# The up-projection of the first batch's second half, made as products of quarters

## The chip, the cores and the metric

The kernel runs on one core of one Trainium2 chip. The metric is the device time of one execution in microseconds (us); the time before is 982.87 us, the median of four runs (981.88 to 982.91).

## The reference

Two blocks follow each other. The first is attention with routing: batch 4, 8 heads, 768 positions, head size 64, 16 clusters. Each query and key goes to its nearest centroid, and a query sees only keys of its own cluster. The second takes the result, transposed to 3072 rows of 512, through two weight matrices.

```python
q_assign = np.argmax(np.einsum('bhsd,hcd->bhsc', q_n, c_n), axis=-1)
k_assign = np.argmax(np.einsum('bhsd,hcd->bhsc', k_n, c_n), axis=-1)
mask = q_assign[:, :, :, None] == k_assign[:, :, None, :]
scores = np.where(mask, scale * np.matmul(q, k.transpose(0, 1, 3, 2)), -1e9)
attn = softmax(scores)                  # rows add up to 1
x = np.matmul(attn, v)                  # -> (3072, 512)
h = x @ w_in                            # w_in 512 x 2048
g = h - np.tanh(h)
return g @ w_out                        # w_out 2048 x 512
```

## The kernel before

**Attention.** Heads are worked in pairs: 4 pairs in each of 4 batches, 16 pairs `n`. A pair is done in two halves of 384 queries (`TB`), and a half in three steps of two key blocks. So there are 96 steps. Steps 0 to 11 are the first halves of the first batch's pairs, 12 to 23 their second halves, 24 to 47 the second batch, 48 to 71 the third, 72 to 95 the fourth. The loop over steps writes all engines' instructions in a hand-made order; nothing is moved afterwards. Each engine takes its instructions strictly in that order.

In every step, `begin` issues 8 score matmul instructions for the following step (`sc`, L451) into two PSUM tiles (pool `ps_s`, two buffers) and two `Exp` on ACT, in place. `value` issues 8 matmul instructions of this step's weights with the values (`av`, L505). `select` (L483) makes the weights of the following step on DVE: it multiplies the exponentials, read from PSUM, by the mask "same code"; it is called twice per step with two instructions each. POOL adds the weights up (`sum`, L492 and L496). In one step of six, a new pair is turned (`pt`, L332), compared with the centroids (`sim`, L351) and routed one step later: `route` transposes (`pr`, L364) and makes codes in four DVE instructions, the last two of which need no PSUM. `publish` (L396, L400) writes the codes to DRAM, from where `spread` fetches them as a row. `total_both` (L566) takes the POOL sums of both halves of a pair through PE.

**The feed-forward block as a filler.** Between these, every step takes some items from a list. The list of the batch before is spread over the steps by weights written by hand (2.6 for an `up`, 3.4 for a `project`). After its matmuls, each item calls `between()`, which emits the next part of the step's `todo` list (the two `select`, then routing, publishing, scaling and so on, split evenly over the items).

- First batch (`plain_items`): 16 `up` items for each half, each 8 matmuls (16 instructions in the profile) of 384 columns (L676), a tanh on ACT (L681) and a subtraction on DVE (L683); then 12 `project` items (L692). First half in steps 12 to 23, second half in steps 24 to 47.
- Later batches (`strassen_items`): the weights and the activations are cut into quarters, and seven products of quarters take the place of eight. `up_product` (L871) makes one product of 4 matmuls (8 instructions) of 384 columns. For each of 8 rows `i` of quarters, the products come in the order 1, 2, 6, 7, 4, 5, 3. Product 1 is copied out of PSUM by ACT (L876); the others are added up by DVE (L859), product 5 in two additions. When two results are ready, `shrink` runs tanh on ACT (L864) and a subtraction on POOL (L866).

All filler matmuls, `sim`, `pr`, `pq` and `den` take turns in the same PSUM pool `ps_f` of three buffers. So a product can begin only when the result three places before it was read.

The sums of weight quarters ("factors") are made by DVE (L773: 8 instructions for the up weights, 8 for the down weights) and kept in DRAM by the SP queue (L737, L756); `light` names the steps for that. `open_stream` (step 39) gives the space of `w_in` to three `stream` buffers, and `fetch_factors` (L795, SP) brings back 896 KB for each row `i`. `right_factors` (L832) makes the differences of activation quarters on DVE.

Of the kernel before, what the change touches and what calls it, by code (L numbers as in the profile page):

```python
# [39 lines left out]
P = 128  # L40
# [18 lines left out]
def kernel(  # L59
# [119 lines left out]
    def fast():  # L179
# [178 lines left out]
        def route(n: int):  # L358

            t = sims.pop(n)  # L360
            ps = ps_f.tile([P, TB], F32, name="pr", tag="f")
            for j in range(HCH):
                c = slice(j * P, (j + 1) * P)
                nc.tensor.transpose(out=ps[:, c], in_=t[:, c], identity=ident)  # L364
            G = HCH * 8
            pr = ps.rearrange("p (g c) -> p g c", c=C)
            shape = [P, G, C]
            places = down.unsqueeze(1).to_broadcast(shape)
            mx = rtp.tile([P, G], F32, name="mx")
            nc.vector.reduce_max(out=mx, in_=pr, axis=AX.X)  # L370
            top = rtp.tile(shape, F32, name="top")
            nc.vector.tensor_tensor(  # L372
                out=top, in0=pr, in1=mx.unsqueeze(2).to_broadcast(shape), op=ALU.is_ge
            )
            nc.vector.tensor_tensor(out=top, in0=top, in1=places, op=ALU.mult)
            code = codes[n] = codep.tile([P, 2, 2, 2, HCH], F32, name="code")
            nc.vector.reduce_max(
                out=code.rearrange("p i a h j -> p j (i a h)"),
                in_=top.rearrange("p (j g) c -> p j g c", j=HCH), axis=AX.X,
            )  # L380
# [238 lines left out]
        def spread_out(n: int, half: int):  # L619
            back = lists.pop((n, half))  # L620
            if joined(n):
                pool = late_pools.get("den", sump)
                dens[n, 1] = pool.tile([P, TB], F32, name="den")
                for i in range(2):
                    for h in range(2):
                        nc.sync.dma_start(
                            dens[n, i][h * D : h * D + D], back[i, h : h + 1].to_broadcast([D, TB])
                        )
                return
            for h in range(2):  # L630
                nc.sync.dma_start(
                    dens[n, half][h * D : h * D + D], back[h : h + 1].to_broadcast([D, TB])
                )
# [31 lines left out]
        def plain_items(half: int):  # L665
# [39 lines left out]
            if half == 0:  # L705

                order = [(s, i) for i in range(NQ4) for s in range(2)] + order[2 * NQ4 :]
            return [(2.6, 1, lambda between, f=f: up(f, between)) for f in sequence] + [
                (3.4, 1, lambda between, s=s, i=i: project(s, i, between)) for s, i in order
# [76 lines left out]
        def fetch_factors(n: int):  # L786

            if n < (B - 1) * PER:
                i = n % PER
                t = streams[n] = late_pools["stream"].tile([P, HF, HM], F32, name="stream")  # L790
                if i < HF:
                    t = streams[n] = t.rearrange("p a b -> p (a b)")[:, 0 : 7 * CH * P].rearrange(
                        "p (c k f) -> p c k f", k=7, c=CH
                    )
                nc.sync.dma_start(t, up_factors[i] if i < HF else down_factors[i - HF])  # L795

        late_pools, diffs = {}, {}

        def open_stream():
            first_in.close()  # L800
            late_pools["stream"] = cx.enter_context(
                tc.tile_pool(name="stream_late", bufs=3, side="right", reuse_waits="tile")
            )
            late_pools["den"] = cx.enter_context(
                tc.tile_pool(name="den_late", bufs=1, side="right", reuse_waits="tile")
            )
            for n in range(2):
                fetch_factors(n)

        def open_late():  # L810
            first.close()
            for name, bufs in (
                ("diff", 1), ("u", 2), ("s", 2), ("th", 2), ("g", 1), ("left", 1), ("du", 1),
                ("c", 4), ("raw", 2),
            ):
                late_pools[name] = cx.enter_context(
                    tc.tile_pool(name=name + "_late", bufs=bufs, reuse_waits="tile")
                )
            late_pools["G"] = late_pools["g"].tile([P, HF, 2, 2, TB], F32, name="G")
            late_pools["S1"] = late_pools["left"].tile([P, HF, TB], F32, name="S1")  # L820

        def right_factors(b: int, c: int):

            if c == 0:
                diffs[b] = late_pools["diff"].tile([P, 3, CH, TB], F32, name="diff")
            d = diffs[b]
            x, y = xT[b * HP + c], xT[b * HP + CH + c]
            for out, u, w in (
                (d[:, 0, c], x[:, 1], x[:, 0]), (d[:, 1, c], y[:, 1], d[:, 0, c]),
                (x[:, 1], y[:, 1], x[:, 1]), (d[:, 2, c], y[:, 0], d[:, 1, c]),  # L830
            ):
                nc.vector.tensor_tensor(out=out, in0=u, in1=w, op=ALU.subtract)  # L832

        def strassen_items(b: int):
            base = (b - 1) * PER

            held = {}
            G, left1 = late_pools["G"], late_pools["S1"]

            def up_product(i: int, k_: int, between):  # L840
                which = PRODUCTS[k_]
                x = [xT[b * HP + c] for c in range(CD)]
                d = diffs[b]
                right = {
                    1: [x[c][:, 0] for c in range(CH)], 2: [x[CH + c][:, 0] for c in range(CH)],
                    3: [x[CH + c][:, 1] for c in range(CH)], 4: [d[:, 2, c] for c in range(CH)],
                    5: [d[:, 0, c] for c in range(CH)], 6: [d[:, 1, c] for c in range(CH)],
                    7: [x[c][:, 1] for c in range(CH)],
                }[which]
                if k_ == 0:  # L850
                    held[i] = (
                        late_pools["s"].tile([P, TB], F32, name="s"),
                        late_pools["u"].tile([P, 2, TB], F32, name="u"),
                    )
                s, u = held[i]
                g = G[:, i]
# [4 lines left out]
                def shrink(f: int, halves_=slice(0, 2)):  # L861
                    t = g[:, f, halves_]
                    th = late_pools["th"].tile([P, 2, TB], F32, name="th")[:, halves_]
                    nc.scalar.activation(out=th, in_=t, func=ACT.Tanh)  # L864
                    t, th = (x.rearrange("p a n -> p (a n)") for x in (t, th))
                    nc.gpsimd.tensor_tensor(out=t, in0=t, in1=th, op=ALU.subtract)  # L866

                ps = ps_f.tile([P, TB], F32, name="pu", tag="f")
# [8 lines left out]
                elif which == 2:  # L877
                    add(g[:, 0, 0], ps, s)
                    if i == HF - 1:
                        shrink(0, slice(0, 1))  # L880
# [5 lines left out]
                elif which == 4:  # L886
                    add(g[:, 1, 0], ps, u[:, 1])
                elif which == 5:
                    add(u[:, 0], ps, u[:, 0])
                    add(g[:, 1, 1], ps, u[:, 1])  # L890
                    shrink(1)
                else:
                    add(g[:, 0, 1], ps, u[:, 0])

                    shrink(0, slice(1 if i == HF - 1 else 0, 2))
                between()
                if k_ == len(PRODUCTS) - 1:

                    nc.gpsimd.tensor_tensor(out=left1[:, i], in0=g[:, 0, 1], in1=g[:, 1, 1], op=ALU.add)
                    nc.gpsimd.tensor_tensor(  # L900
                        out=g[:, 0, 1], in0=g[:, 0, 0], in1=g[:, 0, 1], op=ALU.subtract
                    )
                    streams.pop(base + i)
# [3 lines left out]
            def down_product(k_: int, j: int, between):  # L907
# [51 lines left out]

            return [  # L960
                (1.3, 1, lambda between, i=i, k_=k_: up_product(i, k_, between))
                for i in range(HF) for k_ in range(len(PRODUCTS))
            ] + [
# [11 lines left out]
        def before(n: int):  # L975
# [10 lines left out]
            yield lambda: route(n)  # L986
# [7 lines left out]
        ready = {}  # L994
# [68 lines left out]
        route(0)  # L1063
        turn(1, 0, nc.scalar)
# [13 lines left out]
        route(1)  # L1078
        begin(steps[0])
# [23 lines left out]
        for at, (n, half, s) in enumerate(steps):  # L1103
# [4 lines left out]
            if at == 4 * HALF - 9:  # L1108
                open_stream()
            if at in fills:  # L1110
                fill, over = fills[at][0](), fills[at][1]
                whole, spent, since = sum(it[0] for it in fill), 0.0, at
            if at == 2 * HALF:
                makers = [it for i in range(2) for it in up_maker(i)]
                makers += [it for i in range(2) for it in down_maker(i)]
# [71 lines left out]
            todo += [stages[i] for i in (5, 3, 4, 2) if i in stages]  # L1187
            todo += late
# [18 lines left out]
            light = [i for i in range(at, 4 * HALF - 2) if i % 3 and i % 6 != 1]  # L1207
# [8 lines left out]
            slots = max(sum(it[1] for it in now), 1)  # L1216
            place = iter(range(slots))
# [10 lines left out]
            if at in fills and "raw" in late_pools:  # L1228
# [10 lines left out]

        PRS = len(PRODUCTS)  # L1240
        tail = tail[:2] + tail[PRS : PRS + 2] + tail[2:PRS] + tail[PRS + 2 :]
# [218 lines left out]
```

## Time and profile before

| | us |
|---|---|
| median of four runs | 982.87 |
| the profiled execution, whole | 983.38 |
| its span | 981.6 |
| PE busy in the span | 971.7 |
| DVE, POOL, ACT busy | 535.6, 497.2, 316.6 |
| in the chain: first `h` of step 24, first `o` of step 36 | 206.11, 290.29 |

The page gives busy time per engine, and the costliest groups as "busy, mean ns of one". The view of the chain goes back from the last instruction and says in each stretch what work the end waited for. In the timeline, a bracket holds the idle time before an instruction and what ended it. The granted clock of PE is 0.998 over the span.

### The profile page before, as it was taken

The page shows a single profiled execution, that of the slowest core. Times are in us where ns is not written, and L with a number is a line of the kernel's source. Part 1 is how long each engine was busy: PE and PEld are TensorE (multiplying, and loading weights), DVE is VectorE, ACT ScalarE, POOL GpSimd, SP SyncE. Part 2 cuts the span into 40 slices and gives each one's busy share as a digit, 9 for nine tenths or more (in the row PEclk, how much of TensorE's full clock was granted, in tenths as well). Part 3 has the DMA queues.
Part 4 walks back from the last instruction along what each step waited for, and adds up shares of the span by engine and source line. Part 5 has one row for each costly group of instructions (what it writes and reads, how often), then busy time and mean ns, then how long its engine had stood idle before and what let it go on. Part 6 is the DMA issues. An engine that isn't in the chain of part 4 may idle for free.

```text
span 981.6 us, 16550 instructions
## 1 busy us (share of the span) xinstructions
PE 971.7 (99%) x6456; PEld 460.5 (47%) x6456; DVE 535.6 (55%) x1010; ACT 316.6 (32%) x484; POOL 497.2 (51%) x347
## 2 busy tenths in 40 slices
PE   8999999999999999999999999999999999999997
PEld 5433443344443334444455555444455555444664
DVE  6458656447566577647655457655754436543011
ACT  5576554233332333243422222333242121222000
POOL 1026334444445454677686345666688445466600
PEclk9999999999999999999999999999999999999999
DMA  7664452124565633463544646344344132233221
GB/s 204 183 186 144 151 143 94 30 73 132 155 203 167 173 116 110 148 195 99 180 159 157 188 136 201 110 151 149 123 159 135 62 118 95 83 113 129 104 103 35
DMA packets 113385, 132.47 MB, mean 135 GB/s; under 512 B 60388, under 2 KB 93076, under 8 KB 110612
## 3 DMA queue, kind: packets, MB, share of 16 engines
q1 hardware_dynamic: 106916, 109.81, 36.6%
q0 software_dynamic: 6240, 21.50, 6.3%
q8 instruction: 53, 0.87, 0.4%
q14 instruction: 32, 0.26, 0.1%
q10 hardware_dynamic: 144, 0.03, 0.0%
HBM read 110.14 MB, written 21.17 MB: 134 GB/s over the span
## 4 chain that ended last, share of the span: by engine, by line
PE 95%; DMA 2%; DVE 1%; ACT 1%; SPq 0%; issue 0%; POOL 0%; ACTq 0%; DVEq 0%
PE pd L922 22%; PE pu L871 22%; PE sc L451 14%; PE av L505 13%; PE o L692 8%; PE h L676 8%; PE pt L332 2%; PE sim L351 1%; PE den L566 1%; DMA den<-back 1%; PE den L539 1%; PE den L520 1%; PE pr L364 1%; DVE e L483 1%; DMA row<-q_codes 0%
## 5 line engine op out<-in xcount | busy, mean ns | idle before, releaser
L496 POOL TENSOR_TENSOR sum<-sum,e 128x768 f32<-128x768 f32 x112 | 207.1, 1849 | 100.1 <-DVE e L483 94.2
L483 DVE SCALAR_TENSOR_TENSOR e<-row,code,sc 128x384 f32<-128x384 bf16 x336 | 186.2, 607 | 103.6 <-ACT sc L473 89.3
L473 ACT ACTIVATE sc<-sc 128x768 f32<-128x768 f32 x168 | 125.9, 792 | 216.1 <-PE sc L451 206.4
L922 PE MATMUL pd<-stream,G 128*64 128x256 f32 x1728 | 191.5, 379 | 0.0
L922 PEld LDWEIGHTS pd<-stream,G 128*64 128x64 f32 x1728 | 123.7, 137 | 67.0 <-issue 7.7
L451 PE MATMUL sc<-t,t 64*128 64x384 f32 x768 | 150.2, 509 | 0.6 <-ACT e L473 0.3
L505 PE MATMUL av<-e,vals 128*64 128x384 f32 x768 | 145.6, 498 | 0.5 <-DVE e L483 0.5
L871 PE MATMUL pu<-xT,stream 128*64 128x384 f32 x768 | 134.9, 488 | 0.7 <-DVE top L372 0.7
L866 POOL TENSOR_TENSOR G<-G,th 128x768 f32<-128x768 f32 (+1 forms) x51 | 87.2, 1723 | 94.0 <-ACT th L864 94.0
L871 PE MATMUL pu<-diff,stream 128*64 128x384 f32 x576 | 102.3, 488 | 0.0
L451 PEld LDWEIGHTS sc<-t,t 64*128 64x128 f32 x768 | 65.8, 186 | 75.2 <-issue 40.8
L492 POOL TENSOR_TENSOR sum<-e 128x768 f32<-128x768 f32 x28 | 54.3, 1940 | 77.8 <-DVE e L483 42.1
L871 PEld LDWEIGHTS pu<-xT,stream 128*64 128x64 f32 x768 | 54.1, 137 | 69.5 <-issue 61.8
L864 ACT ACTIVATE th<-G 128x768 f32<-128x768 f32 (+1 forms) x51 | 40.9, 806 | 141.2 <-DVE G L859 141.2
L692 PE MATMUL o<-w_out,g 128*64 128x512 f32 x384 | 86.4, 594 | 0.0
L676 PE MATMUL h<-xT,w_in 128*64 128x384 f32 x512 | 86.3, 487 | 0.0
L505 PEld LDWEIGHTS av<-e,vals 128*64 128x64 f32 x768 | 47.6, 136 | 82.6 <-issue 79.7
L871 PEld LDWEIGHTS pu<-diff,stream 128*64 128x64 f32 x576 | 40.4, 137 | 51.0 <-issue 44.7
L859 DVE TENSOR_TENSOR G<-pu,u 128x384 f32<-128x384 f32 x72 | 39.8, 553 | 43.5 <-PE pu L871 43.5
L676 PEld LDWEIGHTS h<-xT,w_in 128*64 128x64 f32 x512 | 36.4, 137 | 46.2 <-issue 45.1
L933 DVE SCALAR_TENSOR_TENSOR c<-pd,du 128x256 f32<-128x256 f32 x36 | 15.2, 421 | 67.1 <-PE pd L922 67.1
L692 PEld LDWEIGHTS o<-w_out,g 128*64 128x64 f32 x384 | 27.0, 137 | 50.1 <-issue 49.4
(131 smaller groups left out, 828.3 us busy)
## 6 DMA issues: line engine op xcount, KB each, us to landing
stream<-up_factors SPq DMA_DIRECT2D x24, 896.0 KB
stream<-down_factors SPq DMA_DIRECT2D x21, 1024.0 KB
raw<-in_moe_w_in_dram POOLq DMA_DIRECT2D x16, 512.0 KB, 5.3
raw<-in_moe_w_out_dram POOLq DMA_DIRECT2D x16, 512.0 KB, 4.2
again<-in_moe_w_in_dram SPq DMA_DIRECT2D x32, 256.0 KB
again<-in_moe_w_out_dram SPq DMA_DIRECT2D x32, 256.0 KB
x<-in_q_dram SPq DMA_DIRECT2D x32, 192.0 KB
x<-in_k_dram SPq DMA_DIRECT2D x32, 192.0 KB
```

Source lines behind the costliest of these rows:

```text
L451: nc.tensor.matmul(sc[i][:, h, 0:TB], lhsT=turned[n, 1][r].rearrange("p a n -> p (a n)")[:, j * P : (j + 1) * P], rhs=turned[n, 0][r, half ...
L473: nc.scalar.activation(out=out, in_=sc[i][:, :, 0:TB], func=ACT.Exp, scale=SCALE)
L483: nc.vector.scalar_tensor_tensor(out=e[:, h], in0=rows[n, half][:, h], scalar=codes[n][:, 1, j // HCH, h, j % HCH : j % HCH + 1], in1=sc[: ...
L492: nc.gpsimd.tensor_tensor(out=s, in0=pair[0], in1=pair[1], op=ALU.add)
L496: nc.gpsimd.tensor_tensor(out=s, in0=s, in1=pair[i], op=ALU.add)
L505: nc.tensor.matmul(avs[n, half][h * D : h * D + D], lhsT=vals[n][:, h, j], rhs=e[i][:, h], start=(j == 0), stop=(j == NCH - 1),)
L676: nc.tensor.matmul(h[r], lhsT=w_in[i][:, c, o * P : (o + 1) * P][:, r], rhs=xT[c][:, half], start=(c == 0), stop=(c == CD - 1),)
L692: nc.tensor.matmul(acc[sub][r], lhsT=gs[f % HF][:, f // HF, sub * P : (sub + 1) * P][:, r], rhs=w_out[f // FQ][:, f % FQ], start=(f == seq ...
L864: nc.scalar.activation(out=th, in_=t, func=ACT.Tanh)
L866: nc.gpsimd.tensor_tensor(out=t, in0=t, in1=th, op=ALU.subtract)
L871: nc.tensor.matmul(ps[r], lhsT=streams[base + i][:, c, k_, r], rhs=right[c], start=(c == 0), stop=(c == CH - 1),)
L922: nc.tensor.matmul(ps[r], lhsT=left(i)[:, r], rhs=t[:, i], start=(i == 0), stop=(i == HF - 1))
```

## The change

The 16 `up` items of the second half of the first batch become `half_up_items`: 8 rows of seven products, with the 384 queries of the half cut into two quarters of 192 columns. `up_product` is now inside `up_items`, which serves both this half (`b` = 0, width 192) and the later batches (384). For the half, the first two products of rows 0 and 1 come first (`start_without`). Products weigh 0.65, `project` items 3.0.

What goes with it: the up factors are made in steps 20 to 22 instead of steps 26 to 38, the down factors in steps 36 to 46. `open_stream` moves from step 39 to step 23; eight more fetches are made. `den` tiles of steps 24 to 47 lie in a pool of turned tiles. `route` ends after the comparison (its two PSUM reads), and `route_on`, a part of its own in `todo`, makes the codes. In steps 24 to 47, `todo` is filled up with empty parts so that one part is emitted behind each item, the first `select` behind the first product, the second behind the second.

```diff
+        def route_on(n: int):
+            top = tops.pop(n)
+            places = down.unsqueeze(1).to_broadcast([P, HCH * 8, C])
             nc.vector.tensor_tensor(out=top, in0=top, in1=places, op=ALU.mult)
             code = codes[n] = codep.tile([P, 2, 2, 2, HCH], F32, name="code")
             nc.vector.reduce_max(
...
+            ups = [(2.6, 1, lambda between, f=f: up(f, between)) for f in sequence]
+            if half == 1:
+                ups = half_up_items(gs)
...
+                i = n + HF if n < 0 else n % PER
...
+        def columns(b: int, c: int):
+            return xT[b * HP + c] if b else xT[c][:, 1].rearrange("p (a n) -> p a n", a=2)
...
+        def up_items(b: int, base: int, quarter, shrink, done):
+            held = {}
+            width = TB if b else TB // 2
...
+                ps = ps_f.tile([P, TB], F32, name="pu", tag="f")[:, 0:width]
                 for c in range(CH):
                     for r in halves:
                         nc.tensor.matmul(
...
                 if which == 1:
                     nc.scalar.copy(out=s, in_=ps)
                 elif which == 2:
+                    add(quarter(i, 0, 0), ps, s)
...
                 elif which == 5:
                     add(u[:, 0], ps, u[:, 0])
+                    add(quarter(i, 1, 1), ps, u[:, 1])
+                    shrink(i, 1, slice(0, 2))
...
+            return [
+                (1.3 * width / TB, 1, lambda between, i=i, k_=k_: up_product(i, k_, between))
+                for i in range(HF) for k_ in range(len(PRODUCTS))
+            ]
+
+        def start_without(items):
+            n = len(PRODUCTS)
+            return items[:2] + items[n : n + 2] + items[2:n] + items[n + 2 :]
+
+        def half_up_items(gs):
+            W = TB // 2
...
+            def shrink(i: int, f: int, parts):
+                cols = slice(parts.start * W, parts.stop * W)
+                t = gs[i][:, f, cols]
+                th = thp.tile([P, TB], F32, name="th")[:, cols]
+                nc.scalar.activation(out=th, in_=t, func=ACT.Tanh)
+                nc.gpsimd.tensor_tensor(out=t, in0=t, in1=th, op=ALU.subtract)
+            return start_without(up_items(0, -HF, quarter, shrink, lambda i: None))
...
-            if at == 4 * HALF - 9:
+            if at == 2 * HALF - 1:
                 open_stream()
...
+            if at == 2 * HALF - 4:
+                makers = [it for i in range(2) for it in up_maker(i)]
             if at == 2 * HALF:
-                makers = [it for i in range(2) for it in up_maker(i)]
-                makers += [it for i in range(2) for it in down_maker(i)]
+                makers = [it for i in range(2) for it in down_maker(i)]
...
+            if 2 in stages:
+                todo.append(lambda: route_on(routed.pop()))
...
+            if 2 * HALF <= at < 4 * HALF:
+                todo += [lambda: None] * (slots - len(todo))
```

The order that this gives can be read from the built program. Per step from 24 on, the products behind `av` are: 24: row 0's 1 and 2, row 1's 1 and 2, row 0's 6; 25: 7, 4, 5, then `pr`, then 3; 26: 6, 7, 4, 5, 3; 27: 1, 2, 6, `pq`, 7, 4; 28: 5, 3, 1, 2; 29: 6, 7, `den`, 4, 5, `pt`, 3; 30: 1, 2, 6, 7; 31: 4, 5, 3, `pr`, 1, 2; 32: 6, 7, 4, 5, 3; 33: 1, 2, 6, `pq`, 7; 34: 4, 5, 3, 1, 2; 35: 6, 7, `den`, 4, 5, `pt`, 3.

## The prediction

> **What bounds the kernel now.** I read the page first, then the chain of waits stretch by stretch, then the groups by shape and the timeline around the one place where PE waits inside a products stage.
>
> ```profile
> PE 971.7 (99%) x6456; PEld 460.5 (47%) x6456; DVE 535.6 (55%) x1010; ACT 316.6 (32%) x484; POOL 497.2 (51%) x347
> ```
>
> PE carries the span. The chain of the changed stage (start, length, work) shows it without a gap:
>
> ```profile
> 204.62 1.49 PE sc L451 x8
> 206.11 2.73 PE h L676 x16
> 208.84 1.49 PE sc L451 x8
> 210.33 1.44 PE av L505 x8
> 211.77 5.16 PE h L676 x32
> 216.93 0.48 PE pr L364 x3
> ```
>
> 32 instructions of 384 columns take 5.16 us, 161.2 ns each; nothing but PE ends anything. So every PE column saved here is time saved, and every wait that PE gets is time lost. What a products stage does to DVE is shown by the timeline of the second batch, where a step has four products of 384 columns and a `pr`:
>
> ```profile
> 440.99 2.75 PE L871 MATMUL pu<-diff,stream 128*64 128x384 f32 x16
> 442.49 0.56 DVE L859 TENSOR_TENSOR G<-pu,u 128x384 f32<-128x384 f32 x1 [3.54 <-PE pu L871]
> 442.97 1.13 DVE L483 SCALAR_TENSOR_TENSOR e<-row,code,sc 128x384 f32<-128x384 bf16 x2
> 444.01 0.55 DVE L859 TENSOR_TENSOR u<-pu,u 128x384 f32<-128x384 f32 x1
> 444.48 0.55 DVE L859 TENSOR_TENSOR G<-pu,u 128x384 f32<-128x384 f32 x1
> 444.95 1.13 DVE L483 SCALAR_TENSOR_TENSOR e<-row,code,sc 128x384 f32<-128x384 bf16 x2
> 445.99 0.55 DVE L370 TENSOR_REDUCE mx<-pr 128x24 f32<-128x384 f32 x1
> 446.58 0.56 DVE L372 TENSOR_TENSOR top<-pr,mx 128x384 f32<-128x384 f32 x1
> 447.28 1.51 PE L871 MATMUL pu<-xT,stream 128*64 128x384 f32 x8 [0.34 <-DVE top L372]
> ```
>
> DVE stood idle 3.54 us for the first product's addition although exponentials were ready, since the masks (`e`) are queued behind it; then everything came at once, and PE stood 0.34 us for a PSUM buffer. The change puts products half as long on this same chain of additions, masks and three buffers.
>
> **Part 1, fewer columns.** Removed: 16 items of 16 instructions, 256 x 161.2 ns = 41.3 us. Added: 56 products of 8 instructions = 448 of 192 columns. No row has 192. The 256-column row is
>
> ```profile
> 903.11 72.54 PE pd L922 x672
> ```
>
> which is 107.9 ns; the line through 107.9 and 161.2 gives 81 ns at 192, so a product is 0.65 us and all are 448 x 81 = 36.3 us. From below, weight loads: `pt` makes 12 loads of 128 columns with short matmuls in 1.46 us, 122 ns each; two products' loads have as many columns and their matmuls take 162 ns, so loads stay covered. Uncovered they would cost two matmuls 162 + 137 ns, but the 256-column row (216 for two, with the same loads of 137) excludes that. Gain: **5.0 us**. The Trainium skill, "TensorE: Matmul & The Clock Gate", section on the back-to-back issue gap, speaks against: load and matmul together pace the stream, 81 ns at 128 columns and 131 at 512, which would be 89 at 192 and a gain of 1.4 us; its 131 does not agree with the rows here, so I stay with them.
>
> **Part 2, more breaks.** A run of products after `pr` or `pq` begins 0.15 later (2.73 where 16 take 2.58). `pr` and `pq` stood at step ends before `sc` and now stand between products in steps 25, 27, 31 and 33: 4 x 0.15 = **0.6 us**.
>
> **Part 3, new waits of PE.** Prices: an addition of 384 takes 0.555, of 256 (L933) 0.421, so 192 takes 0.36; in a row of instructions the next starts 0.47 later at 384, so 0.27 at 192. Two masks: 1.04 to the next start, 1.13 to the end. From a product's end to its addition 0.21 us (440.99 + 8 x 0.161 to 442.49), from the read of a buffer to PE 0.15 (447.14 to 447.28). Time 0 is the first product after `av`. In general the first addition starts at 0.86, masks at 1.13, second addition at 2.17 (read at 2.53), masks at 2.44 (done 3.57), third addition at 3.48.
> - Steps 26 and 32 (6, 7, 4, 5, 3): the fifth product, due at 2.60, needs the second's buffer at 2.53 + 0.15: 0.1 each. Step 25, with `pr` as the fourth user of a buffer: 0.1.
> - Step 31 (4, 5, 3, `pr`, 1, 2): `pr` takes a buffer, product 5 has two additions, so the third is read at 4.11; the fifth product is due at 4 x 0.65 + 0.63 = 3.23 and starts at 4.26: 1.0.
> - Step 34 (4, 5, 3, 1, 2): the second buffer is read at 2.80, 2.95 against 2.60: 0.35.
> - Step 28 (5, 3, 1, 2): only four products; the next step's second score tile, due at 3.4, waits for the second masks, done at 3.84: 0.6.
> - Step 27 (1, 2, 6, `pq`, 7, 4): ACT's exponentials queue behind two tanh that wait for step 26's last additions; the third addition is read at 3.18, the fifth product is due at 2.96: 0.4.
> - Steps 29 and 35: `den` needs POOL's sums. POOL now has 15 subtractions of 1.00 and 2 of half that width in its queue, in front of sums of 1.85; in step 28 two subtractions end at 4.35, two sums at 8.05, and `den`, which came at 7.43, starts at 8.2: 0.8 (0.4 after step 34). Then the second masks come behind the third addition, and `pt` waits for their score buffer: 0.4 each. Together 2.0.
> - Steps 24, 30, 33 begin with a product that ACT copies, so masks start early: 0.
>
> Sum **4.5 us**. From below: the only row of such a wait is 0.34 for a step with `pr`, two of those are 0.7. From above: instructions that do not overlap at all (0.36 and 1.13 in full) make the same list 7.2. I take 4.5, as the timeline's pitch fits its own nine lines. The Trainium skill, "VectorE: DVE Perf Modes", section on the TRN2 errata, says the same of small tiles: 120 cycles fixed and one per element from PSUM at 0.96 GHz, by which an addition of 192 is an estimated 0.325 us and a step's waits shrink by under 0.1.
>
> **Part 4, what is moved and hidden.** The makers' 8 DVE instructions sum to 11.5 us in L773's `w_in` groups; they go from steps 26 to 38 to steps 20 to 22 (162 to 192 us), where DVE is busy 15.95 of 30:
>
> ```profile
> 162.00:172.00 10.00, 10.00 (x54) 3.49 (x50) 6.91 (x11) 4.91 (x9) 2.88 (x2) 1.00 0.31 101
> 172.00:182.00 10.00, 10.00 (x51) 3.42 (x49) 5.51 (x9) 2.54 (x5) 5.93 (x5) 1.00 0.18 46
> 182.00:192.00 10.00, 10.00 (x52) 3.56 (x52) 3.53 (x5) 1.70 (x3) 4.01 (x3) 1.00 0.07 28
> ```
>
> The masks queued behind them end near 187 instead of 184.65, and `av` needs them at 191.98: 0. Their 28 DMAs of 256 KB go ahead on SP of the fourth pair's codes and row (177.45 and 178.75 now, some 185 then; needed at 192.3) and of the next pair's loads. DMA moved 277 GB/s from 232 to 236 us, so 7.3 MB take 27 us. The last is issued at about 192; two `stream` fetches of 0.9 MB behind it land near 203, and PE asks at 206.1 and 207.4: 0, with 3 us of cover; if DVE or SP comes 5 us late, 2 us are lost. `right_factors` (8 x 0.27 = 2.2 us) fits in DVE's 7.44 idle us before 206.39. Dropped tanh (16 x 0.488) and added copies and tanh cancel on ACT within 3 us, off the path. `den` tiles, down factors in steps 36 to 46 and `route_on` lie where the chain has no DVE at all: 0.
>
> **Sum.** -5.0 + 0.6 + 4.5 = +0.1 us on a profiled execution of 983.38 (span 981.6 and 1.8 around it), which lies 0.5 above the median. So 983.0 us: the columns saved come back as waits.
>
> **Rivals.** (a) *The gain stays.* If additions and masks run ahead as they do in the second batch, where only `pr` steps wait, waits are 0.7 to 2.5 and the change brings 1.9 to 3.7 us: 979.2 to 981. For it: DVE has only 24 x 1.13 + 56 x 0.36 = 47 us of masks and additions in some 80. Against: order, not load, makes the waits, and 0.65 is shorter than addition plus half of the masks. (b) *The queue behind the first addition costs more than the products save.* One mechanism, in steps 25 to 35: with no overlap between DVE's instructions the waits are 7.2, net +2.8, 985.7; it is slower by over 0.2% from 6.4 us of waits on. For it: L483's mean is 607 ns against 565 in the timeline above. (c) *The streams are late* in step 24 because make, keep and fetch follow each other within 35 us: +2 to 5 on top of the sum, 985 to 988. Against: 3 us of cover.
>
> **How the numbers follow.** No measurable change, which for this kernel is within 0.2% (2 us): 0.39, own range 981.0 to 984.9. Rival a 0.28, b 0.20, c 0.13. The range reaches from rival a's better half to the middle of c: 979.7 to 987.0. Faster 0.28, same 0.39, slower 0.33.
>
> **What would show it.** Right: 8 products' instructions at 81 ns where they run without a wait; idle time of PE before `pu`, `sc` and `den` "<-DVE" and "<-POOL" of 4 to 5 us in steps 25 to 35, most in 28, 29, 31 and 35; no wait for a DMA at step 24. Wrong: 192-column instructions at 88 ns or more (part 1), waits under 2.5 us (rival a), a gap before the first product (c), or a stage after step 36 that is longer than before.

## The result and the profile after

The changed kernel takes 985.04 us (median of 33 runs, 984.26 to 986.07); the kernel before takes 982.88 us (53 runs). The ratio is 1.0022 with a 95% interval of 1.0017 to 1.0027. Forecast was 983.0 us, with 979.7 to 987.0 as the range. So the time is inside the range and 2 us above the number. The change makes the kernel 2.16 us slower, 0.22%, at the edge of the 0.2% that the forecast had called no change (the interval reaches down to 0.17%).

In the profiled execution the span went from 981.6 to 983.1 us. The granted clock is 0.999, so none of it is the throttle. The page's first part, after:

```profile
PE 970.5 (99%) x6648; PEld 472.9 (48%) x6648; DVE 547.7 (56%) x1058; ACT 318.8 (32%) x493; POOL 513.9 (52%) x364
```

PE works 1.2 us less than the 971.7 of before, and the span is 1.5 us longer: PE waits more. The view of the chain tells where. Between the first product of step 24 and the first `o` of step 36 the kernel before takes 84.18 us (206.11 to 290.29), the changed one 84.73 (205.83 to 290.56). That is 0.55 us more. The rest of the loss is elsewhere, in two steps that the prediction had put at nothing.

**Inside the stage.** Products that wait for nothing run as forecast. The view of the chain, after; columns are start, duration, what:

```profile
205.83 3.40 PE pu L887 x40
...
218.39 3.30 PE pu L887 x40
...
290.56 3.58 PE o L700 x16
```

The last line is the first `o` of step 36. The second line is step 26: 40 instructions in 3.30 us of which about 0.05 is its small wait, so 81 ns each. The first is step 24, which begins with no wait for the streams. The worst new wait is in step 31:

```profile
253.67 0.67 PE pu L887 x8
...
254.65 1.13 DVE e L488 x2
255.78 0.27 DVE t L882
...
256.23 1.13 DVE e L488 x2
257.36 0.28 DVE g L882
...
257.68 0.87 PE pu L887 x8
```

Read it as DVE's queue in order: behind the first product's addition the first mask (two `e`), two additions, the second mask, and only then, at 257.36, the addition for product 3. The step's order on PE is 4, 5, 3, `pr`, 1, 2. When product 2 is due, 3, `pr` and 1 hold all three buffers of `ps_f`, so it waits for that addition and starts at 257.68.

**Outside the stage.** Step 49 is the second step of the third batch's stage. The chain there, before and then after:

```profile
384.42 2.58 PE pu L871 x16
387.00 0.48 PE pr L364 x3
387.48 2.73 PE pu L871 x16
```

```profile
384.70 1.31 PE pu L887 x8
...
386.97 2.18 DVE e L488 x4
389.15 0.48 DVE G L882
...
389.68 1.51 PE pu L887 x8
```

Before, both ends of this stretch lie on PE, 5.79 us from 384.42 to the next scores at 390.21. After, it is 6.49 us (384.70 to 391.19). All four mask instructions (2.18 us) stand in one piece ahead of an addition that PE needs. The same happens at 618.23 us, in the fourth batch, with the same 6.49 against 5.79.

The account of the two profiled executions: -0.28 us at the start of step 24 (the two differ by that already at 140 us), +0.55 in the stage, +0.70 twice. The sum is 1.67 us. The last DVE instruction lies at 975.68 before and at 977.34 after, 1.66 later, so nothing else moved the time. The -0.28 is scatter between executions: an experiment below that edits the kernel before only from step 48 on starts step 24 at 205.54. Without it the traces show 1.95 us of loss, of the 2.16 between the medians.

### The profile page after: what moved, and what is told of

It reads as the page before. It is cut to its first block, busy times and chain, and to the rows that moved or that the text cites. A ratio compares the mean times of both kernels' runs of the same rounds, so it can differ in the third digit from the quotient of the medians.

```text
span 983.1 us, 17054 instructions
## 1 busy us (share of the span) xinstructions
PE 970.5 (99%) x6648; PEld 472.9 (48%) x6648; DVE 547.7 (56%) x1058; ACT 318.8 (32%) x493; POOL 513.9 (52%) x364
## 4 chain that ended last, share of the span: by engine, by line
PE 93%; DVE 3%; DMA 3%; issue 1%; SPq 0%; ACT 0%; POOL 0%; DVEq 0%; ACTq 0%
PE pu L887 24%; PE pd L983 22%; PE sc L456 13%; PE av L510 13%; PE o L700 8%; PE h L684 4%; PE pt L332 2%; DVE e L488 2%; PE sim L351 1%; DMA den<-back 1%; PE den L571 1%; PE den L544 1%; PE den L525 0%; PE pr L364 0%; DMA x<-in_k_dram 0%
## 5 line engine op out<-in xcount | busy, mean ns | idle before, releaser
L501 POOL TENSOR_TENSOR sum<-sum,e 128x768 f32<-128x768 f32 x112 | 209.3, 1868 | 90.6 <-DVE e L488 86.5
L887 PE MATMUL pu<-xT,stream 128*64 128x384 f32 (+1 forms) x1024 | 160.7, 449 | 2.5 <-DVE G L882 1.0
L887 PE MATMUL pu<-diff,stream 128*64 128x384 f32 (+1 forms) x768 | 120.9, 448 | 0.2 <-DVE t L882 0.2
L887 PEld LDWEIGHTS pu<-xT,stream 128*64 128x64 f32 x1024 | 71.3, 137 | 78.0 <-issue 64.2
L887 PEld LDWEIGHTS pu<-diff,stream 128*64 128x64 f32 x768 | 53.7, 137 | 57.0 <-issue 48.4
L994 DVE SCALAR_TENSOR_TENSOR du<-pd,du 128x256 f32<-128x256 f32 x27 | 11.4, 421 | 60.3 <-PE pd L983 60.3
L684 PE MATMUL h<-xT,w_in 128*64 128x384 f32 x256 | 42.9, 487 | 0.0
```

What stands on the lines that cost most here:

```text
L501: nc.gpsimd.tensor_tensor(out=s, in0=s, in1=pair[i], op=ALU.add)
L684: nc.tensor.matmul(h[r], lhsT=w_in[i][:, c, o * P : (o + 1) * P][:, r], rhs=xT[c][:, half], start=(c == 0), stop=(c == CD - 1),)
L887: nc.tensor.matmul(ps[r], lhsT=streams[base + i][:, c, k_, r], rhs=right[c], start=(c == 0), stop=(c == CH - 1),)
```

## The experiments

The theory after the result had two parts. First, `route_on` as a part of its own costs 0.70 us in each of two steps, because the list of a step is split evenly over its items, and one part more moves both masks into one slot. Second, inside the stage, DVE's order costs as much as the products save: the masks stand behind the first products' additions. The rivals: the cost outside the stage belongs to the quarters (pools, streams, space), and inside the stage to load on DVE or POOL, not to order.

### The codes in one part again, from the third batch on

```diff
             if 2 in stages and at < 4 * HALF:
                 todo.append(lambda: route_on(routed.pop()))
+            elif 2 in stages:
+                todo.append(lambda whole=todo.pop(): (whole(), route_on(routed.pop())))
```

> The changed kernel, but from step 48 on the codes are made behind the comparison in one part of the step's list, as before the change; steps 0 to 47 keep the two parts. Theory (the extra part shifts the even split of the list, so that in the second step of the third and the fourth batch's stages both masks come in one slot, 2.18 us in a row, ahead of an addition whose buffer PE needs): the two waits of 0.7 us go, 985.0 becomes 983.6. Rival (those waits come from the products of quarters, by the changed load of POOL and ACT or by the eight more transfers): the time stays at 985.0.

Measured: 983.58 us, ratio to before 1.0008 (0.9999 to 1.0017). The chain of this kernel has the step of before again:

```profile
384.83 2.58 PE pu L887 x16
387.41 0.48 PE pr L364 x3
387.89 2.73 PE pu L887 x16
```

1.46 us come back, two times 0.70 and a rest within the scatter.

### The kernel before, with only the codes in two parts

The other way round: nothing of the quarters, `route_on` alone.

```diff
+            if 2 in stages:
+                todo.append(lambda: route_on(routed.pop()))
```

> The kernel before with one edit alone: the codes of a pair are made in two places (the comparison in one part of the list, the place and the maximum in a part of their own), as in the changed kernel; no quarters, no filling up with empty parts. Theory: the extra part shifts the even split of the list over the items, so that in one step of the third and one of the fourth batch both masks (four instructions, 2.18 us) stand in one slot ahead of an addition that PE waits for; it costs 0.70 us in each, and perhaps once more in the second batch: 882.9 is not touched otherwise, so 982.9 + 1.4 = 984.3 us, up to 985.0 if the second batch's step is hit as well. Rival: the cost belongs to the quarters (space, pools, streams) and not to the split: 982.9 us.

Measured: 984.73 us, ratio 1.0015 (1.0006 to 1.0024). Its chain shows the wait in step 49, and the same at 618.02 us; the stage of steps 24 to 35 keeps its 84.18 us (206.16 to 290.34):

```profile
384.48 1.31 PE pu L876 x8
...
386.76 2.18 DVE e L488 x4
...
389.46 1.51 PE pu L876 x8
```

So the cost belongs to the split of the list, not to the quarters. The median is 1.7 above before; the traces account for 1.4 of it. The second batch, which the expectation held possible, is not hit: from step 24 to step 49 this kernel takes 178.32 us, the kernel before 178.31.

### Masks ahead of the products, in the stage only

```diff
+            masks_first = []
+            if following and 2 * HALF <= at < 3 * HALF:
+                masks_first = todo[:ahead_of]
+                todo[:ahead_of] = [lambda: None] * ahead_of
...
+            for it in masks_first:
+                it()
             for it in now:
                 it[2](between)
```

`ahead_of` is 2, and 1 in steps 29 and 35, where `den` stands between the masks.

> The changed kernel, but in steps 24 to 35 the two masks are emitted ahead of the products instead of behind the first and second one (in steps 29 and 35 only the first mask, as the second has to follow the sums' way through PE); all else keeps its place. The work is the same. Theory (PE's 4.8 us of waits come from the order on DVE: masks stand behind the first addition, later additions behind the masks, POOL's sums behind the masks): about 1 us of waits is left, mostly the score buffer in steps 29 and 35, and 985.0 becomes 981.2. Rival (the waits are load: DVE and POOL have too much to do in that stage, whatever the order): the time stays within 0.5 us of 985.0. Second rival (masks that wait for ACT's exponentials now hold up the additions behind them): 986 or more.

Measured: 981.86 us, ratio 0.9991 (0.9982 to 1.0000). The stage shrinks from 84.73 to 81.48 us, with the same instructions on every engine. The waits of steps 27, 28, 31 and 34 are gone; only the order changed, so order made them, not load. The trace gives back 3.25 us of the 3.8 expected; what is left, and what is new, is in steps 24, 29 and 35 (below).

### Masks ahead of the products, in all steps from 24 on

The same edit with `at >= 2 * HALF`.

> The changed kernel with the masks ahead of the items in all steps from 24 on. Theory: besides the 3.8 us of steps 24 to 35 the waits of the later batches go, 0.7 us in each of two steps (codes in two parts) and 1.86 us in each of two steps with routing that the kernel before had too: 985.0 - 3.8 - 1.4 - 3.7 = 976.1. Rival (in the later batches masks ahead of products of 384 columns wait for exponentials behind two tanh of 0.84 us and hold the additions up): above 979.

Measured: 979.80 us, ratio 0.9966 (0.9954 to 0.9978). It is faster than both kernels. Step 31 is free of waits:

```profile
253.18 1.95 PE pu L887 x24
255.13 0.48 PE pr L364 x3
255.60 1.45 PE pu L887 x16
```

The expectation of 976.1 was too low, and the chain says why. It counted two old waits of 1.86 us each, in steps of the third and fourth batch that are the same in both kernels. In the kernel before, the first of them (step 55) runs from 441.15 to 448.80 us. The same step here:

```profile
439.13 2.58 PE pu L887 x16
441.71 0.48 PE pr L364 x3
442.19 4.02 PE pu L887 x24
```

40 instructions of `pu`: the step has five products, not the four that I had counted. Without a wait it takes 7.08 us, with it 7.65, so each of those waits is worth 0.57. Two of them and the 1.4 of `route_on` make 2.5; 2.1 was measured on top of the kernel with the edit in the stage only.

### The kernel before, masks ahead of the products from the third batch on

The same edit in the kernel before, with `at >= 4 * HALF`.

> The kernel before the change, with the masks ahead of the items in all steps from 48 on; no products of quarters in the first batch. Theory: only its own two waits of 1.86 us go, 982.9 becomes 979.2; against the run with products of quarters and masks first, the quarters are then worth 3 us, their 5.0 us less breaks and what waits are left. Rival (the order of the masks does nothing in the later batches): 982.9.

Measured: 981.92 us, ratio 0.9987 (0.9978 to 0.9996). It has the same miscount in its expectation: two waits of 0.57 go, 1.1 us, and 1.0 was measured. This kernel is the fair partner for the quarters: 979.80 against 981.92. With the masks in the right place, the quarters bring 2.1 us between the medians, where 3 was expected; by the intervals of the two ratios it could be off by over 1 us. The two traces put it at 2.70, a stage of 84.18 us (205.54 to 289.72) against 81.48.

### The changed kernel without the empty parts

```diff
-            if 2 * HALF <= at < 4 * HALF:
-                todo += [lambda: None] * (slots - len(todo))
```

> The changed kernel without the empty parts in steps 24 to 47, so that the parts of a step are split evenly over its items: with five products and two masks the first mask comes behind the third product, the second behind the fifth. Theory (order on DVE decides): the second mask of a step ends near 4.9 us after the first product instead of 3.6, the score buffer that it reads is needed at 3.4, so about 1.3 us more of waits in six of the twelve steps, some in the others: about 8 us more, 993 us (990 to 997). Rival (load on DVE decides, the order within a step does not): 985.0 us, within 1.

Measured: 993.55 us, ratio 1.0105 (1.0090 to 1.0121). In the chain of this kernel even step 24, which waits for nothing in the changed kernel, now stands still before the scores of the next step:

```profile
205.71 1.48 PE pu L887 x16
...
209.99 0.61 DVE e L488
...
210.65 0.92 PE sc L456 x4
```

The second half of the scores starts at 210.65, right behind the mask that frees its buffer; in the changed kernel all eight instructions run from 209.23 on, half of them by 209.98. The stage takes 93.08 us (205.71 to 298.79) where the changed kernel takes 84.73. The same work in a third order costs 8.5 us, the largest effect of the study. "Load decides" is refuted from this side too.

### The changed kernel without POOL's subtractions in the stage

```diff
                 nc.scalar.activation(out=th, in_=t, func=ACT.Tanh)
-                nc.gpsimd.tensor_tensor(out=t, in0=t, in1=th, op=ALU.subtract)
```

> The changed kernel with POOL's subtractions of the second half of the first batch left out (activation h instead of h - tanh(h), tanh still made). Theory, as in the prediction: the waits of den in steps 29 and 35 (PE in the den row 1.39 and 1.53 us instead of 0.78) come from subtractions that stand in front of the sums in POOL's queue; without them the 0.6 in step 29 goes, and of the 0.75 in step 35 at least the 1.0 of the subtraction in front of the sums, so 985.0 - 1.35 = 983.7 us. Rival: den in step 35 waits for the sums alone, which run from the second mask of step 34 on (277.3 + 3.7): half of it stays, 984.3 us; or the waits just move to pt: 985.0 us.

Measured: 983.83 us against 985.04. The stage takes 83.39 us (205.15 to 288.54), 1.34 less. The rows of `den` in the changed kernel and here:

```profile
239.05 1.39 PE den L571 x8
281.48 1.53 PE den L571 x8
```

```profile
238.38 0.78 PE den L571 x8
280.20 0.78 PE den L571 x8
```

Both waits, 0.61 and 0.75 us, are POOL's queue: subtractions in front of the sums that `den` reads.

### The subtractions on DVE instead of POOL, masks first

```diff
-                nc.gpsimd.tensor_tensor(out=t, in0=t, in1=th, op=ALU.subtract)
+                nc.vector.tensor_tensor(out=t, in0=t, in1=th, op=ALU.subtract)
```

> The changed kernel with the masks first in all steps from 24 on (as in the run before this one), and the subtractions behind the tanh of the second half of the first batch on DVE instead of POOL. Theory: the wait left in step 35 (PE idle until 280.6 us, the first mask at 279.17 behind three POOL subtractions that end at 279.07) is POOL's queue of sums and subtractions; without the subtractions POOL is done near 276, and about 1.5 us of wait goes: 979.8 - 1.5 = 978.3 us. DVE gets 24 instructions of 0.27 to 0.47 us more, 10 us in a stage of 82. Rival 1: the first mask waits for the exponentials or the row of the next pair, not for POOL: 979.8 us. Rival 2: the subtractions on DVE stand in front of additions and give the gain back: 980 to 981 us.

Measured: 986.71 us, ratio 1.0027 (1.0008 to 1.0045); 6.9 us slower than masks first alone, far beyond all three expectations. The timeline of DVE in step 25 shows two costs at once:

```profile
214.95 0.35 DVE L882 TENSOR_TENSOR g<-pu,t 128x192 f32<-128x192 f32 x1
215.89 1.11 DVE L942 TENSOR_TENSOR g<-g,th 128x384 f32<-128x384 f32 x1 [0.59 <-ACT th L941]
```

First, an addition hands over to ACT's tanh, and the subtraction behind it waits 0.59 us for that tanh at the head of DVE's queue. Everything behind it waits too, the additions and the masks that PE needs among them. The stage has 17 such subtractions (the expectation had 24), and DVE stands idle 10.2 us in front of them. Second, this subtraction takes 1.11 us, where nine of its size take 0.56. Six begin while a sum of POOL runs, and they take 1.11 to 2.09 us; all 17 take 14.9 us, where 10 were expected. The stage is 89.06 us long (206.09 to 295.15) against 81.48. No run separates the two costs. On POOL, the same subtractions waited for the same tanh without such a loss. The experiment says nothing on what it was made for, the wait left in step 35 with masks first.

### The wait left in step 35, by two further edits

With masks first, the trace names POOL as what releases the first mask of step 35. The kernel with masks first in all steps, DVE's timeline:

```profile
274.33 2.05 DVE L646 TENSOR_TENSOR xT<-xT,den 128x384 f32<-128x384 f32 x1
276.31 1.35 DVE L646 TENSOR_TENSOR xT<-xT,t 128x384 f32<-128x384 f32 x1
277.58 0.34 DVE L882 TENSOR_TENSOR g<-pu,t 128x192 f32<-128x192 f32 x1
279.17 1.14 DVE L488 SCALAR_TENSOR_TENSOR e<-row,code,sc 128x384 f32<-128x384 bf16 x2 [1.24 <-POOL g L942]
```

But ACT's timeline has another candidate that ends at the same moment:

```profile
278.02 0.36 ACT L941 ACTIVATE th<-g 128x192 f32<-128x192 f32 x1 [2.76 <-DVE g L882]
278.29 1.49 ACT L478 ACTIVATE sc<-sc 128x768 f32<-128x768 f32 x2
```

The exponentials that the mask multiplies stand behind a tanh, which waits for the addition at 277.58, which stands behind two scalings of `xT`. One kernel leaves out POOL's subtractions (the edit shown above), the other moves the scalings by one step:

```diff
-                        later.setdefault(at + i, []).append(
+                        later.setdefault(at + i - (at + i == 3 * HALF - 2 and i == 5), []).append(
```

> The kernel with the masks first in all steps from 24 on, and POOL's subtractions behind the tanh of the second half of the first batch left out (that half's activation is then h, not h - tanh(h); the tanh itself is still made). It is compared with 979.8 us, the time of the kernel with the masks first. Theory 1: the wait left in step 35 comes from ACT's order: the exponentials of step 36's scores, that the first mask needs, stand behind a tanh that waits for an addition behind two scalings of xT on DVE (2.05 and 1.35 us, where such an instruction takes 0.55 alone); POOL's sums (272.25 to 275.97) still slow the first scaling, so the wait shrinks by 0.8 us at most: 979.0 to 979.8. Theory 2: the mask waits for the three subtractions in POOL's queue, as the releaser in the trace says: the wait of 1.5 us goes, 978.3 us.

> The kernel with the masks first in all steps from 24 on, and one more edit: the two scalings of xT (DVE) that stood in step 34, ahead of the last addition of that step, stand at the end of step 33. Nothing on POOL, ACT or PE is moved. Theory 1 (ACT's exponentials behind tanh behind addition behind scalings): the addition of step 34 comes 3.2 us earlier, tanh and exponentials with it, and the wait of step 35 goes: 979.8 - 1.3 = 978.5 us, with the first mask of step 35 at 277.5 or before in place of 279.17. Theory 2 (the three subtractions in POOL's queue): 979.8 us, the mask still right behind POOL's last subtraction. If the scalings run into POOL's sums in step 33 and hold up the masks of step 34: 980 us or more.

Measured: 978.79 us without the subtractions, 979.02 with the scalings moved (ratio 0.9957, 0.9943 to 0.9972). Both lose the same wait: the stage takes 81.09 us in each, 0.39 less than with masks first alone. DVE's timeline with the scalings moved:

```profile
268.68 1.05 DVE L646 TENSOR_TENSOR xT<-xT,den 128x384 f32<-128x384 f32 x1
269.65 0.55 DVE L646 TENSOR_TENSOR xT<-xT,t 128x384 f32<-128x384 f32 x1
277.34 1.14 DVE L488 SCALAR_TENSOR_TENSOR e<-row,code,sc 128x384 f32<-128x384 bf16 x2 [2.33 <-ACT sc L478]
```

In all three kernels the mask starts 0.88 us behind the start of its exponential: 278.29 and 279.17 with masks first, 276.45 and 277.33 without the subtractions, 276.46 and 277.34 with the scalings moved. In the last, POOL's subtractions are all still there and run to 277.66, past the start of the mask. So the mask waits for ACT's exponential, and that POOL ended at 279.07, just ahead of the mask, was a coincidence. What holds the tanh in front of the exponential differs: with masks first it starts at 278.02, behind the addition that ends at 277.92; with the scalings moved the addition ends at 275.02, but the tanh starts at 276.19, and its timeline names POOL's first subtraction, which ends at 276.16. There PE no longer waits for it. Leaving the subtractions out helps because the second scaling then takes 0.55 us in place of 1.35. Both expectations of the gain were off in size: I had put the wait at 1.3 to 1.5 us, and it was worth 0.39. In the medians alone, 979.02 and 979.80 can't be told apart for sure, since their intervals overlap; the 0.39 rests on the traces. With 979.02 us the kernel with the scalings moved beats both the kernel before and the changed one.

## Why the prediction was right and wrong

The kernel with masks first and the scalings moved has a stage almost without waits. Left are 0.26 us in step 24 (3.66 us from the first product to the scores, 3.40 in the changed kernel), and a wait of `pt` in steps 29 and 35, where the second mask stays behind `den`. The second six `pt` need the score buffer that this mask reads. DVE's timeline and the chain in step 35:

```profile
280.68 1.13 DVE L488 SCALAR_TENSOR_TENSOR e<-row,code,sc 128x384 f32<-128x384 bf16 x2
```

```profile
281.01 0.80 PE pt L332 x6
281.81 0.10 issue
281.91 0.84 PE pt L332 x6
```

The mask ends at 281.81, and the next `pt` starts at 281.91; in step 29 it is 241.41 and 241.52. In step 35 of the changed kernel without POOL's subtractions the mask ends 0.60 us behind the first `pt` in place of 0.80, and the twelve run without a gap:

```profile
282.65 1.52 PE pt L332 x12
```

So some 0.23 us of the 1.75 that `pt` takes in the kernel with the scalings moved are a wait. This is read from the traces; no run moved that mask alone. The stage's bare length is then 81.09 - 0.26 - 2 x 0.23 = 80.37 us. With that, each part can be measured by itself.

**Part 1, fewer columns: right.** 448 instructions at 81 ns, as drawn from the rows of 256 and 384 columns. The Trainium skill, "TensorE: Matmul & The Clock Gate", section "Back-to-back issue gap", would make it an estimated 89 ns, by interpolation between its 128 and 512 columns; 16 instructions in 1.30 us (the first line below) decide for 81.

**Part 2, breaks: mis-sized by about 0.6 us.** Bare, the stage lost 84.18 - 80.37 = 3.81 us, where I had 5.0 - 0.6 = 4.4. I counted breaks only at `pr` and `pq`. The products are also cut by `den` and `pt`, which lay behind the last `h` of a step before. The chain of the kernel with the scalings moved, step 29:

```profile
237.08 1.30 PE pu L887 x16
238.38 0.78 PE den L571 x8
239.16 1.45 PE pu L887 x16
...
242.36 0.80 PE pu L887 x8
```

16 instructions take 1.30 us behind `av` and 1.45 behind `den`; 8 take 0.80 behind `pt` instead of 0.65. That is eight breaks of 0.15, not four. Four more breaks are 0.6 us. `pt` without its wait went from 1.46 to 1.52 us in each of the two steps, another 0.1, and `av` behind a product is 0.15 shorter in each, 0.3 back. That makes 0.4 of the 0.6 that is missing; the runs of products without a break, 1.95 us for 24, give 36.4 us for all columns in place of 36.3, another 0.1.

**Part 3, waits: right in mechanism and size.** 84.73 - 80.37 = 4.4 us were waits, forecast 4.5 (the prediction's own list adds up to 4.65). Against the kernel with the scalings moved, step by step: 25, 26 and 32: 0.07, 0.04, 0.05 (forecast 0.1 each); 27: 0.42 (0.4); 28: 0.60 (0.6); 31: 1.00 (1.0); 34: 0.40 (0.35); 24, 30 and 33: no wait (0). For steps 29 and 35 together I had 2.0, and 1.8 was measured: 0.59 and 0.73 more than in that kernel, and the 0.46 that this kernel still has there itself. `den` behind POOL's sums is 0.61 and 0.75 of it (forecast 0.8 and 0.4), shown by leaving the subtractions out. `pt` waits 0.2 in each, 1.72 us against 1.52 (forecast 0.4 each).

The stage came out at +0.55 against +0.1 because of Part 2; inside Part 3 the errors on `den` and `pt` partly cancel. That the time fell inside the range is luck in part: 985.0 lies above the 984.9 to which the prediction's own reading reached, where the range stood open for rivals b and c, more waits in the stage or late streams, and neither came.

**Part 4, what is moved and hidden: the failed step.** The streams and makers cost nothing, as forecast: from 142 us to step 24 the chains before and after take the same 63.46 us, from step 36 to step 48 the same 84.60. But "`route_on` lie where the chain has no DVE at all: 0" was wrong. It costs 0.70 us twice, shown from both sides, by taking it out and by putting it alone into the kernel before. I asked where its own two instructions would lie. I did not ask what one more entry in `todo` does to the slots of the others, in steps far from the change, although the even split is one line of the loop. The prediction's last part did name "a stage after step 36 that is longer than before" as what would show it wrong, and that is what the trace shows.

**Rivals.** Rival a (waits of 0.7 to 2.5) and rival b (7.2) are refuted by 4.4; rival c by step 24, whose first product starts at 205.83, no later than before. The slower side came out by a mechanism that none of them had: 1.40 of the 1.95 us in the traces lie in the two steps of `route_on`.

## What to carry to other kernels

Where engines take work strictly in the order written, price a new entry in a list by what it does to the slots of its neighbours, not by its own duration; compare the order of every engine in every stage, also those the change does not name. When a stage's products get shorter, work with a deadline (here the masks that free the score buffers) goes ahead of the first product in the helper engine's queue, and work that waits on a third engine (here a subtraction behind a tanh) stays out of that queue. To size a wait, compare the step with the same step in a kernel without it, and see that it has none there too; the gap in the timeline, or a nominal length with a miscounted product, gave 1.86 for 0.57 and 1.5 for 0.39.

## What the hardware showed unexpectedly

The same DVE instruction, a product of two SBUF tiles of 128x384 in fp32 (the scaling of `xT`), takes 0.55 us alone and up to 2.17 us beside POOL's sums. The changed kernel, DVE and then POOL:

```profile
278.26 2.17 DVE L646 TENSOR_TENSOR xT<-xT,t 128x384 f32<-128x384 f32 x1
```

```profile
277.88 4.23 POOL L501 TENSOR_TENSOR sum<-sum,e 128x768 f32<-128x768 f32 x2
```

One by one, the sums run from 277.88 to 280.01 and from 280.09 to 282.11, 2.13 and 2.02 us, where the median of such sums is 1.82. The DVE instruction begins during the first sum and ends at 280.43, 0.42 us behind it. The same distance returns in the kernel with the subtractions on DVE, which also have two SBUF inputs: the six that begin during a sum take 1.11 to 2.09 us, and each ends 0.41 to 0.43 us behind that sum; the nine others of that size take 0.56. DVE's additions with one input from PSUM, 0.34 to 0.36 us for 192 columns, show nothing of it. The Trainium skill, "SBUF — State Buffer", section "SBUF: two separate sides", has a rule for it: DVE with two SBUF inputs and POOL reading SBUF contend for one shared pair of ports, and the later one is blocked for the whole instruction. The rows agree for DVE: however early its instruction begins, it ends a fixed time behind POOL's. For POOL they agree less sharply: both sums are longer, by 0.31 and 0.20 us, the first beside the scaling that still runs until 278.34, the second beside the end of the next one. No run here measured the two alone.
